# A convolution on TensorE in eight 64x32 tiles instead of four of full height, for the second 512 tokens of a fused convolution and gated network

## The chip, the cores and the metric

The kernel runs on one core of a Trainium2 chip. The metric is device time in microseconds for one launch, as the median over runs. A profile is one execution taken by the hardware profiler; its span runs from the first to the last instruction of the program.

## The reference

Eight sequences of 4096 tokens with 192 channels go through a causal depthwise convolution of seven taps, with the softmax of the weights as taps and one set of taps for each head of 24 channels. The result, 32768 tokens, goes through a gated network with 1536 hidden units.

```python
def _attn_ref(x, weight):
    ...                                   # w: softmax of weight over its 7 taps
    x_pad = np.concatenate([np.zeros((B, pad, D)), x], axis=1)      # pad = 6
    idx = np.arange(S)[:, None] + np.arange(K)[None, :]
    x_unf = x_pad[:, idx, :].reshape(B, S, K, H, group)
    out = np.einsum('hk,bskhg->bshg', w, x_unf)
    ...

def _moe_ref(x, w_gate, w_val, w_out):
    gate = np.maximum(x @ w_gate, 0.0)
    val = x @ w_val
    return gate * val @ w_out
```

## The kernel before

The kernel works on sixteen units of 1024 tokens, of two sequences at once (streams 0 and 1, in partitions 0 to 63 and 64 to 127), so a unit has two windows of 512 tokens. Three chunks of 64 channels (`NCH`) hold the 192 channels. For a window, `gate_val` goes over twelve blocks `f` of 128 hidden units: six matmuls with `Wg` and six with `Wv` (line 550), each half with the rows of one stream; then ACT takes the relu of the gate (line 561), and DVE multiplies with the value (line 562). The hidden activations are projected with `Wo` (lines 579, 628, 658) and written out.

The convolved tokens stand in `xc`. From unit 1 on DVE, ACT and POOL compute them in lanes, beside TensorE's work on the unit before. For unit 0 nobody had time, so TensorE does it: the stationary operand is a piece of raw tokens (`x_h`: tokens in partitions, channels along), the moving operand a band matrix (`band`) that holds the taps of one head along its diagonals. `first_block` convolves the first 512 tokens before the first products, `second_block` the second 512 tokens; the latter is called from `gate_val` between blocks 4 and 5 of the first window, so that PE meets it in program order right behind the matmuls of block 4. Both use `conv_dense` (line 370): a window is cut in five pieces of at most 104 tokens, which with six tokens of history fill 110 rows; for each chunk and piece there are two rounds of four matmuls, one for each 32 output channels (two streams, two halves of the chunk), at column places 0, 32, 64 and 96 of the array, all four into one PSUM bank. A second round is needed because 32 channels touch two heads: it overwrites the channels of the other head. So the block is 3 x 5 x 8 = 120 matmuls. ACT moves two chunks from PSUM to `xc` (line 394), DVE the third (line 396).

The order of instructions on each engine is the program's own: nothing reorders it (`tc.manual_schedule()`), and waits follow from data and buffers. PSUM is a pool of four tiles `ps` of two banks, used in turn by everything on TensorE.

POOL issues the transfers that change the type: tokens `x_h` for the first window (lines 134, 135), for the second (line 96, `load_x(1)`, one transfer per stream, two in all) and for the group behind (`load_x(2)`), weights `Wg` and `Wv` in six pieces (line 170). The weights arrive in partitions 0 to 63; DVE copies the first two pieces into partitions 64 to 127, POOL the others (lines 177 and 186). In POOL's order `load_x(1)` stands between pieces 2 and 3 of the weights. Piece 2 is for blocks 3 and 4, piece 3 for blocks 5 and 6, piece 4 for 7 and 8, piece 5 for 9 to 11. [...] Behind the weights POOL issues the raw tokens of unit 1 (line 208).

Of the kernel before, what the change touches and what calls it, by code (L numbers as in the profile page):

```python
# [17 lines left out]
def kernel(  # L18
# [12 lines left out]
    nc = tc.nc  # L31

    B, S, D = x.shape
    H, KW = weight.shape
    G = D // H
    DFF = moe_w_gate.shape[1]
    PAD = KW - 1
    NB = B // 2
# [3 lines left out]
    WIN = 512  # L42
    NWIN = S // WIN
    SUB = 112
# [2 lines left out]
    FOR_POOL = [(1, 6), (2, 6)]  # L47
    GSUB = 5
    DSUB = 104


    UNIT = 2 * WIN
# [4 lines left out]
    TDVE = (LDVE + HALO) // 128  # L57
    FIRST = WIN - DSUB * (GSUB - 1)
    GROUPS = [(0, [0] + [FIRST + DSUB * j for j in range(GSUB - 1)])]
    GROUPS += [(0, [WIN + DSUB * j for j in range(GSUB)])]  # L60
    GROUPS += [(0, list(range(UNIT + LDVE, 2 * UNIT, SUB)))]

    ctx.enter_context(tc.manual_schedule())
# [10 lines left out]
    psum = ctx.enter_context(tc.tile_pool(name="psum", bufs=4, space=bass.MemoryType.PSUM))  # L74
    dram = ctx.enter_context(tc.tile_pool(name="dram", bufs=2, space=bass.MemoryType.DRAM))

    ROOM = 4 * WIN

    def x_room():
        flat = xpool.tile([128, ROOM], F16, name="x_h")  # L80
        return flat[:, 0 : GSUB * 2 * D].rearrange("p (j s d) -> p j s d", j=GSUB, s=2)


    def load_x(g):


        bp, toks = GROUPS[g]
        n, rows, step = len(toks), SUB if g < 2 else 128, toks[1] - toks[0]
        xt = xts[g] = x_room()
        for st in range(2):  # L90
            src = bass.AP(
                tensor=x.tensor,
                offset=x.offset + ((bp + NB * st) * S + toks[0] - PAD) * D,
                ap=[[D, rows], [step * D, n], [1, D]],
            )
            nc.gpsimd.dma_start(out=xt[0:rows, 0:n, st, :], in_=src)
            yield
# [7 lines left out]
    xts = {}  # L105
    ROWS0 = DSUB + PAD
    SEG = 16
# [5 lines left out]
    def stage(p0, rows, st, n_st, jj, n):  # L113
        at = room[p0 : p0 + rows, 0, 0, 0:1]
        dims = [[D * GSUB, n_st], [D, n], [1, D]]
        return bass.AP(
            tensor=at.tensor,
            offset=at.offset + D * (GSUB * st + jj),
            ap=[at.ap[0]] + [d for d in dims if d[1] > 1],
        )  # L120

    xts[0] = x_room()

    def body(st):
        return bass.AP(
            tensor=x.tensor,
            offset=x.offset + (NB * st * S + FIRST - PAD) * D,
            ap=[[D, SUB], [DSUB * D, GSUB - 1], [1, D]],
        )
# [6 lines left out]
        out=xts[0][PAD : PAD + FIRST, 0, :, :],  # L136
        in_=bass.AP(
            tensor=x.tensor, offset=x.offset, ap=[[D, FIRST], [NB * S * D, 2], [1, D]]
        ),
# [35 lines left out]
    def both_halves(copy, s, dst):  # L175
        cols = slice(CUTS[s], CUTS[s + 1])
        copy(out=dst[64:128, :, cols], in_=dst[0:64, :, cols])
# [49 lines left out]
    load_w(1)  # L227
    load_w(2)
    load_rest(load_x(1))
    load_w(3)  # L230
    pool_parts(2)
# [9 lines left out]
    def bits(src, n, down, keep):  # L241
        out = const.tile([SUB, n], I32, name=f"bits{down}")
        nc.vector.tensor_scalar(
            out=out[:],
            in0=src,
            scalar1=down,
            scalar2=keep,
            op0=ALU.logical_shift_right,
            op1=ALU.bitwise_and,
        )  # L250
        return out
# [4 lines left out]
    col = bits(steps[:, 0:NROW], NROW, 0, 63)  # L256
# [3 lines left out]
    with nc.allow_low_precision("zero and one"):  # L260
        nc.vector.tensor_tensor(
            out=same[:], in0=col[:, 0:SEG], in1=s_of[:].to_broadcast([SUB, SEG]), op=ALU.is_equal
        )
        nc.vector.tensor_scalar(
            out=places[:, SUB - SEG : SUB - SEG + NROW],
# [7 lines left out]
        out=mx[:], in_=wr[:], axis=mybir.AxisListType.X, op=ALU.max, negate=True  # L273
# [6 lines left out]
    with nc.allow_low_precision("rounded as the band is"):  # L280
        nc.vector.tensor_scalar(
            out=soft[:],
# [7 lines left out]
        out=spread[0:SUB, 0, 0:H],  # L290
        lhsT=soft[:].rearrange("h k s -> h (k s)"),
        rhs=same[0:H, 0:H],
        start=True,
        stop=True,
# [3 lines left out]
    with nc.allow_low_precision("products with one and zero"):  # L298
        nc.vector.tensor_tensor(
            out=diag[:],  # L300
# [6 lines left out]
    for a in range(2):  # L307
        for b in range(NSEG):
            nc.tensor.matmul(  # L309
                out=(bps, spread)[a][:, a, HB * SEG * b : HB * SEG * (b + 1)],  # L310
                lhsT=places[:, SUB - SEG * (b + 1) : SUB - SEG * (b + 1) + 128],
                rhs=diag[:, HB * a : HB * (a + 1), :].rearrange("p h s -> p (h s)"),
                start=True,
                stop=True,
                skip_group_check=True,
# [4 lines left out]
    for cols in (slice(0, 64), slice(64, D)):  # L320
        nc.scalar.copy(
            out=xts[0][0:ROWS0, 1:GSUB, 0, cols],
            in_=stage(0, ROWS0, 0, 1, 1, GSUB - 1)[:, :, cols],
# [22 lines left out]
    def band(h):  # L346
        return bands[h]

    xc = {}
# [3 lines left out]
    def conv_dense(g, c, ps, bank):  # L353


        xt = xts[g]
        toks = GROUPS[g][1]
        t0 = toks[0]
        ends = toks[1:] + [t0 + WIN]
        for jj in (1, 2, 3, 4, 0):  # L360
            col, n = toks[jj] - t0, ends[jj] - toks[jj]
            rows = n + PAD
            for second in range(2):
                for st in range(2):
                    for k2 in range(2):
                        k = 2 * c + k2
                        h0, h1 = 32 * k // G, (32 * k + 31) // G
                        h, m = (h0, G * h1 - 32 * k) if second else (h1, 32)
                        p0 = 64 * st + 32 * k2
                        nc.tensor.matmul(  # L370
                            out=ps[p0 : p0 + m, bank, col : col + n],
                            lhsT=xt[0:rows, jj, st, 32 * k : 32 * k + m],
                            rhs=band(h)[0:rows, 0:n],
                            start=True,
                            stop=True,
                            tile_position=(0, p0),
                            skip_group_check=True,
                        )

    def first_block():  # L380
        xc[0] = xcpool.tile([128, NCH, UNIT], F16, name="xc")
        both_halves(nc.vector.tensor_copy, 0, Wg)
        both_halves(nc.vector.tensor_copy, 0, Wv)
        for c in range(NCH):
            ps = psum.tile([128, 2, 512], FP, name="ps")
            conv_dense(0, c, ps, 0)
            copy = nc.vector.tensor_copy if c == 2 else nc.scalar.copy
            copy(out=xc[0][:, c, 0:WIN], in_=ps[:, 0, :])

    def second_block():  # L390
        two, one = [psum.tile([128, 2, 512], FP, name="ps") for _ in range(2)]
        conv_dense(1, 0, two, 0)
        conv_dense(1, 1, two, 1)
        nc.scalar.copy(out=xc[0][:, 0:2, WIN : 2 * WIN], in_=two[:])
        conv_dense(1, 2, one, 0)
        nc.vector.tensor_copy(out=xc[0][:, 2, WIN : 2 * WIN], in_=one[:, 0, :])

    HEADS = (((0, 1), (3, 4)), ((6, 7), (2, 5)))

# [389 lines left out]


    first_block()
    taps = const.tile([H, KW], FP)
    nc.scalar.activation(taps[:], ex[:, 0:KW], ACTF.Copy, scale=sm[:])
    tap = const.tile([128, NCH, KW], FP)
    for h in range(H):
        r = G * h
        while r < G * (h + 1):
            c, n = r // 64, min(64 - r % 64, G * (h + 1) - r)
            nc.sync.dma_start(
                out=tap[r % 64 : r % 64 + n, c, :],  # L800
                in_=taps[h : h + 1, :].unsqueeze(1).to_broadcast([1, n, KW]),
# [8 lines left out]
    load_rest(lane_load(1))  # L810
    nc.gpsimd.tensor_copy(out=tap[64:128], in_=tap[0:64])
    load_rest(load_x(2))
    for end in ends:
        nc.gpsimd.memset(end, 0.0)
    load_rest(lane_turn(1))
    for u in range(NUNIT):
# [35 lines left out]
        if u + 1 < NUNIT:  # L852
            begun = lane_first(u + 1)
            if u == 0:
                flat = ypool.tile([128, ROOM], F16, name="y")
                y = flat[:, 0 : GSUB * NCH * 128].rearrange("p (j c s r) -> p j c s r", j=GSUB, c=NCH, s=2)
# [43 lines left out]
```

## Time and profile before

| what | value |
|---|---|
| median of 3 runs | 762.16 us (761.86 to 766.11) |
| span of the profiled execution | 759.9 us; its own time with what lies around the span isn't listed apart, the median of the runs is 2.2 us longer |
| PE busy | 756.1 us, 99% |
| DVE, ACT, POOL busy | 93%, 81%, 53% |
| first and second convolution on PE in the chain | 1.95 us and 1.62 us |
| unit 0 on PE | until 56.82 us |
| a later unit on PE | 46.6 us (from 56.82 to 103.56 us, for instance) |

A row of the timeline has the start in us, the length from the first start to the last end, the engine, the line, the operation, output and input, and how many instructions were merged. Brackets hold idle time of the engine before, and what ended it. PEld is the loading of the stationary operand, which runs beside PE. "Busy" of PE counts matmuls from start to a modelled end, and they overlap, so the spacing of starts says more than the duration of one.

### The profile page before, as it was taken

The numbers are of one execution on the slowest core, as the hardware profiler recorded it, in microseconds if no ns is written. First come the engines' busy times: TensorE is split into PE (matmuls) and PEld (weight loads), VectorE is DVE, ScalarE is ACT, GpSimd is POOL, SyncE is SP. The second block draws the span as 40 slices with busy tenths as digits, with TensorE's granted clock in tenths as the row PEclk, the third lists the DMA queues.
The fourth block names the chain that finished last, engine by engine and source line by source line (L and its number), as shares of the span: only waits on it lengthen the run. The fifth ranks groups of instructions, "written<-read, shape, count | busy, mean of one in ns | idle before, by whom it ended". The sixth has DMA issues, their size and how long they took to land.

```text
span 759.9 us, 30608 instructions
## 1 busy us (share of the span) xinstructions
PE 756.1 (99%) x13623; PEld 484.0 (64%) x13623; DVE 707.4 (93%) x768; ACT 617.3 (81%) x719; POOL 404.9 (53%) x263
## 2 busy tenths in 40 slices
PE   9999999999999999999999999999999999999998
PEld 5495555555666666666666666666666776666548
DVE  7998999999999999999999999999999999999891
ACT  6887887978879798897988879788798887976671
POOL 9519449094580936819276291863908548091000
PEclk9999999999999999999999999999999999999999
DMA  9969029688395894949759498594957939654732
GB/s 118 132 113 136 16 68 157 162 107 181 94 184 146 91 180 105 190 128 105 195 93 184 119 138 180 81 186 114 170 145 100 189 98 160 140 107 113 185 87 85
DMA packets 231308, 100.33 MB, mean 132 GB/s; under 512 B 185288, under 2 KB 220424, under 8 KB 231176
## 3 DMA queue, kind: packets, MB, share of 16 engines
q1 hardware_dynamic: 189928, 82.71, 53.1%
q0 software_dynamic: 41104, 15.57, 20.7%
q8 instruction: 106, 1.74, 1.0%
q14 instruction: 26, 0.21, 0.1%
q10 hardware_dynamic: 144, 0.10, 0.0%
HBM read 31.48 MB, written 47.19 MB: 104 GB/s over the span
## 4 chain that ended last, share of the span: by engine, by line
PE 99%; ACT 0%; issue 0%
PE ps L550 66%; PE ps L658 29%; PE ps L579 3%; PE ps L628 1%; PE ps L154 0%; PE ps L370 0%; PE ps L309 0%; PE ps L411 0%; ACT acc L605 0%; PE ps L289 0%
## 5 line engine op out<-in xcount | busy, mean ns | idle before, releaser
L562 DVE TENSOR_TENSOR hT<-gr,ps 128x1024 f16<-128x1024 f16 (+1 forms) x386 | 469.0, 1216 | 30.0 <-ACT gr L561 3.3
L561 ACT ACTIVATE gr<-ps 128x1024 f16<-128x1024 f32 (+1 forms) x386 | 393.3, 1020 | 100.7 <-PE ps L550 100.3
L498 POOL TENSOR_TENSOR prods<-prods 128x1344 f32<-128x1344 f32 x70 | 212.9, 3042 | 268.7 <-DVE prods L494 265.3
L550 PE MATMUL ps<-xc,Wg 64*64 64x512 f16 (+1 forms) x4320 | 321.9, 376 | 0.0
L550 PE MATMUL ps<-xc,Wv 64*64 64x512 f16 (+1 forms) x4320 | 321.6, 376 | 0.0
L658 PE MATMUL ps<-hT,Wo 64*64 64x512 f16 x4032 | 220.3, 376 | 0.0
L550 PEld LDWEIGHTS <-Wg 64*64 64x64 f16 (+1 forms) x4320 | 154.0, 106 | 94.9 <-issue 0.7
L550 PEld LDWEIGHTS <-Wv 64*64 64x64 f16 (+1 forms) x4320 | 152.7, 105 | 95.8 <-issue 0.3
L658 PEld LDWEIGHTS <-Wo 64*64 64x64 f16 x4032 | 140.2, 107 | 77.4
L522 DVE SCALAR_TENSOR_TENSOR acc<-x_r,tap,acc 128x576 f32<-128x576 f16 x225 | 165.3, 814 | 0.0
L492 ACT ACTIVATE prods<-x_r,tap 128x448 f32<-128x448 f16 x222 | 127.2, 659 | 0.0
L680 ACT COPY x_h<-ps 128x2048 uint16<-128x2048 uint16 x28 | 51.8, 1848 | 8.8 <-PE ps L658 8.8
L208 POOL DMA_DIRECT2D x_e<-in_x_dram x58 | 46.9, 818 | 12.3 <-ACT acc L508 12.0
L472 POOL COPY x_p<-x_e 128x960 f16<-128x960 f16 (+1 forms) x58 | 50.5, 912 | 0.5 <-DMA x_e<-in_x_dram 0.5
L498 POOL TENSOR_TENSOR xc<-prods 128x1344 f16<-128x1344 f32 x14 | 42.5, 3037 | 1.1
L680 POOL COPY y<-x_h 128x2048 uint16<-128x2048 uint16 x14 | 26.6, 1897 | 23.3 <-ACT x_h L736 23.3
L522 DVE SCALAR_TENSOR_TENSOR xc<-x_r,tap,acc 128x576 f16<-128x576 f16 x45 | 34.1, 813 | 0.0
L508 ACT ACTIVATE acc<-x_r,tap 128x576 f32<-128x576 f16 x45 | 31.4, 765 | 0.0
L494 DVE TENSOR_SCALAR prods<-x_r,tap 128x448 f32<-128x448 f16 x70 | 27.7, 448 | 0.0
L579 PE MATMUL ps<-Wo,hT 64*128 64x192 f16 x576 | 24.6, 243 | 0.0
L579 PEld LDWEIGHTS <-hT 64*128 64x128 f16 x576 | 23.9, 94 | 0.5
L736 ACT COPY x_h<-ps 128x512 f32<-128x512 f32 x14 | 8.2, 587 | 10.9 <-ACT x_h L680 5.5
(62 smaller groups left out, 91.6 us busy)
## 6 DMA issues: line engine op xcount, KB each, us to landing
out_dram<-out_s SPq DMA_DIRECT2D x62, 384.0 KB
held<-x_h SPq DMA_DIRECT2D x14, 512.0 KB
held<-x_h SPq DMA_DIRECT2D x28, 256.0 KB
held<-y SPq DMA_DIRECT2D x14, 512.0 KB
x_e<-in_x_dram POOLq DMA_DIRECT2D x34, 192.0 KB, 6.7
x_e<-in_x_dram POOLq DMA_DIRECT2D x24, 240.0 KB, 5.4
x_r<-x_p SPq DMA_TRANSPOSE x131
out_s<-held SPq DMA_TRANSPOSE x56
```

The costliest lines, as they stand in the source:

```text
L208: first = nc.gpsimd.dma_start(out=xe[:, j0 + start : j0 + n, st, :, :].rearrange("p j c r -> p j (c r)"), in_=bass.AP(tensor=x.tensor, off ...
L472: nc.gpsimd.tensor_copy(out=xp[:, j0 : j0 + n, :, st, :], in_=xe[:, j0 : j0 + n, st, :, :])
L492: engine.activation(out=out, in_=in_, func=ACTF.Copy, scale=scale)
L498: nc.gpsimd.tensor_tensor(out=pr[:, 0] if k < KW - 1 else xc[v + 1][:, :, LDVE:UNIT], in0=pr[:, 0], in1=pr[:, k], op=ALU.add,)
L508: nc.scalar.activation(out=accs[v][:, c, :], in_=shifted(v, c, 0, 0), func=ACTF.Copy, scale=tap[:, c, 0:1],)
L522: nc.vector.scalar_tensor_tensor(out=xc[v][:, c, 0:LDVE] if k == KW - 1 else acc[:, c, :], in0=shifted(v, c, k, 0), scalar=tap[:, c, k : k ...
L550: nc.tensor.matmul(out=pss[i][m : m + M, st, :], lhsT=W[64 * st : 64 * st + 64, c, 128 * f + m : 128 * f + m + M], rhs=xcb[64 * st : 64 * ...
L561: nc.scalar.activation(out=gr[:, sts], in_=pss[0][:, sts], func=ACTF.Relu)
L562: nc.vector.tensor_tensor(out=h[:, f, sts], in0=gr[:, sts], in1=pss[1][:, sts], op=ALU.mult)
L579: mm = nc.tensor.matmul(out=outs[q], lhsT=h[64 * r : 64 * r + 64, f, st, 128 * q : 128 * (q + 1)], rhs=Wo[64 * r : 64 * r + 64, f, :], sta ...
L658: mm = nc.tensor.matmul(out=ps[bank][64 * half : 64 * half + 64], lhsT=Wo[64 * r : 64 * r + 64, f, d : d + 64], rhs=hs[w][64 * r : 64 * r ...
L680: copy(out=pt[:], in_=src[:].bitcast(U16).rearrange("p b (t l) -> p b l t", l=2))
```

## The change

The second window is cut in six pieces of 43 tokens in each half of 256 tokens. A piece with its history is 49 rows, and the two halves stand in partitions 0 to 48 and 64 to 112 of one buffer. For each chunk and piece there are two rounds of eight matmuls, four column places times two row halves. Row half 0 writes into bank 0, row half 1 into bank 1, so a PSUM tile holds the first 256 tokens of two chunks in one bank and the last 256 in the other. The moving operand for row half 1 is the band matrix from its row 64 and column 64 on, which has the same diagonals. That is 3 x 6 x 16 = 288 matmuls, and 288 loads. The two copies out of PSUM read and write in strips of 256 tokens. `load_x(1)` issues four transfers, one per stream and half. The buffers for raw tokens grow from 2048 to 2304 elements per partition.

```diff
+    HSUB, NHS = 43, 6
+    HROWS = HSUB + PAD
...
-    GROUPS += [(0, [WIN + DSUB * j for j in range(GSUB)])]
+    GROUPS += [(0, [WIN + HSUB * j for j in range(NHS)])]
...
-    ROOM = 4 * WIN
+    ROOM = NHS * 2 * D
...
         xt = xts[g] = x_room()
+        if g == 1:
+            for st in range(2):
+                for r in range(2):
+                    src = bass.AP(
+                        tensor=x.tensor,
+                        offset=x.offset + (NB * st * S + toks[0] + WIN // 2 * r - PAD) * D,
+                        ap=[[D, HROWS], [step * D, n], [1, D]],
+                    )
+                    nc.gpsimd.dma_start(out=xt[64 * r : 64 * r + HROWS, 0:n, st, :], in_=src)
+                yield
+            return
...
+    def conv_split(c, ps, col0):
+        xt = xts[1]
+        for jj in range(NHS):
+            n = min(HSUB, WIN // 2 - HSUB * jj)
+            col = col0 + HSUB * jj
+            for second in range(2):
+                for st in range(2):
+                    for k2 in range(2):
+                        k = 2 * c + k2
+                        h0, h1 = 32 * k // G, (32 * k + 31) // G
+                        h, m = (h0, G * h1 - 32 * k) if second else (h1, 32)
+                        p0 = 64 * st + 32 * k2
+                        for r in range(2):
+                            rows = slice(64 * r, 64 * r + n + PAD)
+                            nc.tensor.matmul(
+                                out=ps[p0 : p0 + m, r, col : col + n],
+                                lhsT=xt[rows, jj, st, 32 * k : 32 * k + m],
+                                rhs=band(h)[rows, 64 * r : 64 * r + n],
+                                start=True,
+                                stop=True,
+                                tile_position=(64 * r, p0),
+                                skip_group_check=True,
+                            )
...
     def second_block():
         two, one = [psum.tile([128, 2, 512], FP, name="ps") for _ in range(2)]
-        conv_dense(1, 0, two, 0)
-        conv_dense(1, 1, two, 1)
-        nc.scalar.copy(out=xc[0][:, 0:2, WIN : 2 * WIN], in_=two[:])
-        conv_dense(1, 2, one, 0)
-        nc.vector.tensor_copy(out=xc[0][:, 2, WIN : 2 * WIN], in_=one[:, 0, :])
+        half = WIN // 2
+        conv_split(0, two, 0)
+        conv_split(1, two, half)
+        nc.scalar.copy(
+            out=xc[0][:, 0:2, WIN : 2 * WIN].rearrange("p c (r t) -> p c r t", r=2),
+            in_=two[:].rearrange("p r (c t) -> p c r t", c=2),
+        )
+        conv_split(2, one, 0)
+        nc.vector.tensor_copy(
+            out=xc[0][:, 2, WIN : 2 * WIN].rearrange("p (r t) -> p r t", r=2), in_=one[:, :, 0:half]
+        )
```

On POOL, between pieces 1 and 4 of the weights, before (sizes are partitions x runs x elements; `x2` counts equal rows in a row):

```order
L170 DMA Wg<-in_moe_w_gate_dram 64x3x256
L170 DMA Wv<-in_moe_w_val_dram 64x3x256
L96 DMA x_h<-in_x_dram 112x5x192 x2
L170 DMA Wg<-in_moe_w_gate_dram 64x3x256
L170 DMA Wv<-in_moe_w_val_dram 64x3x256
L177 COPY Wg<-Wg 64x3x256
L186 COPY Wv<-Wv 64x3x128 x2
```

and now:

```order
L183 DMA Wg<-in_moe_w_gate_dram 64x3x256
L183 DMA Wv<-in_moe_w_val_dram 64x3x256
L100 DMA x_h<-in_x_dram 49x6x192 x4
L183 DMA Wg<-in_moe_w_gate_dram 64x3x256
L183 DMA Wv<-in_moe_w_val_dram 64x3x256
L190 COPY Wg<-Wg 64x3x256
L199 COPY Wv<-Wv 64x3x128 x2
```

Two more token transfers, each with about half as many rows, stand ahead of piece 3 of the weights and of the copies of piece 2; the rest of POOL's order is as before.

On PE, the start of the second convolution behind block 4 (a matmul reads the band and the loaded tokens; the size is output channels x tokens), before:

```order
L550 MATMUL ps<-xc,Wv 128x512
L370 LDWEIGHTS x_h
L370 MATMUL ps<-band_182,x_h 32x104
L370 LDWEIGHTS x_h
L370 MATMUL ps<-band_182,x_h 32x104
```

and now:

```order
L595 MATMUL ps<-xc,Wv 128x512
L409 LDWEIGHTS x_h
L409 MATMUL ps<-band_184,x_h 32x43
L409 LDWEIGHTS x_h
L409 MATMUL ps<-band_184,x_h 32x43
```

The place in PE's order is the same; four such pairs made a round, and now eight pairs do, with 43 columns for 104. PE has 168 matmuls and 168 loads more in all.

More of the change, by code (lines that the diff above doesn't have):

```diff
@@ L75 @@
     dram = ctx.enter_context(tc.tile_pool(name="dram", bufs=2, space=bass.MemoryType.DRAM))
-    ROOM = 4 * WIN
+    ROOM = NHS * 2 * D
     def x_room():
         flat = xpool.tile([128, ROOM], F16, name="x_h")
-        return flat[:, 0 : GSUB * 2 * D].rearrange("p (j s d) -> p j s d", j=GSUB, s=2)
+        return flat[:, 0 : NHS * 2 * D].rearrange("p (j s d) -> p j s d", j=NHS, s=2)
     def load_x(g):
         bp, toks = GROUPS[g]
-        n, rows, step = len(toks), SUB if g < 2 else 128, toks[1] - toks[0]
+        n, rows, step = len(toks), 128, toks[1] - toks[0]
         xt = xts[g] = x_room()
+        if g == 1:
[9 more added lines that the diff above has]
+            return
         for st in range(2):
```

## The prediction

> **What bounds the kernel now.** I read the page first: engine shares and the chain that ended last.
>
> ```profile
> span 759.9 us, 30608 instructions
> PE 756.1 (99%) x13623; PEld 484.0 (64%) x13623; DVE 707.4 (93%) x768; ACT 617.3 (81%) x719; POOL 404.9 (53%) x263
> PE 99%; ACT 0%; issue 0%
> ```
>
> TensorE is the bound from end to end. The other engines matter only where they make PE wait, and PE never catches up a delay, since it has next to no idle time. So the question is local: when does PE leave the changed block and what follows it? The chain in order of time (start, length, what) shows its place:
>
> ```profile
> 7.23 6.74 PE ps L550 x60
> 13.97 1.62 PE ps L370 x113
> 15.59 24.71 PE ps L550 x228
> 56.82 31.20 PE ps L550 x576
> ```
>
> The changed convolution (L370, second call) is 1.62 us of 759.9, 0.2%. No saving in it can exceed that. The timeline of the first 22 us has its neighbours: gate and value products L550 of blocks 3 and 4 (Wg, then Wv), the convolution, block 5, and the Wv half of block 9.
>
> ```profile
> 11.09 0.94 PE L550 MATMUL ps<-xc,Wg 64*128 64x512 f16 x6
> 11.74 0.94 PE L550 MATMUL ps<-xc,Wv 64*128 64x512 f16 x6
> 12.39 0.94 PE L550 MATMUL ps<-xc,Wg 64*128 64x512 f16 x6
> 13.10 0.87 PE L550 MATMUL ps<-xc,Wv 64*128 64x512 f16 x6
> 13.90 1.69 PE L370 MATMUL ps<-band,x_h 110*32 110x104 f16 x120
> 15.07 1.01 ACT L394 CAST xc<-ps 128x1024 f16<-128x1024 f32 x1 [0.68 <-PE ps L370]
> 15.53 0.82 PE L550 MATMUL ps<-xc,Wg 64*128 64x512 f16 x6
> 15.68 0.69 DVE L396 CAST xc<-ps 128x512 f16<-128x512 f32 x1
> 16.18 0.81 PE L550 MATMUL ps<-xc,Wv 64*128 64x512 f16 x6
> 21.36 0.81 PE L550 MATMUL ps<-xc,Wv 64*128 64x512 f16 x5
> ```
>
> In the same stretch POOL issues the token transfer (L96) and, behind it on the same queue, the weight transfers (L170) and the copies of weights into partitions 64 to 127 (L177, L186), which PE needs:
>
> ```profile
> 6.06 0.63 POOL L170 DMA_DIRECT2D Wv<-in_moe_w_val_dram  x1
> 6.68 1.64 POOL L96 DMA_DIRECT2D x_h<-in_x_dram  x2
> 8.31 0.65 POOL L170 DMA_DIRECT2D Wg<-in_moe_w_gate_dram  x1
> 9.63 0.82 POOL L177 COPY Wg<-Wg 64x768 f16<-64x768 f16 x1
> 10.97 0.95 POOL L186 COPY Wv<-Wv 64x384 f16<-64x384 f16 x2 [0.52 <-DMA Wv<-in_moe_w_val_dram]
> 11.87 0.64 POOL L170 DMA_DIRECT2D Wg<-in_moe_w_gate_dram  x1
> 13.76 0.82 POOL L177 COPY Wg<-Wg 64x768 f16<-64x768 f16 x1
> 14.53 0.83 POOL L177 COPY Wv<-Wv 64x768 f16<-64x768 f16 x1
> 19.63 1.16 POOL L177 COPY Wv<-Wv 64x1152 f16<-64x1152 f16 x1
> 20.73 0.88 POOL L208 DMA_DIRECT2D x_e<-in_x_dram  x1
> ```
>
> The reader should compare ends with starts: the Wg copy for blocks 3 and 4 ends at 9.63 + 0.82 = 10.45, PE wants it at 11.09, a slack of 0.64 us. The last Wv copy ends at 20.79 and is wanted at 21.36, a slack of 0.57.
>
> **Term 1, the matmuls.** Before: 120 matmuls of up to 104 columns in the 1.62 us of the chain (13.90 to 15.52 in the timeline), 30 steps of four column tiles. What a column costs comes from the long rows: 576 matmuls of 512 columns in 31.20 us are 54 ns each, with four 64x64 tiles at work 217 ns for 512 columns, 0.42 ns a column. (That row also shows two row halves at work together, each into its own bank.) A step of 512/5 = 102 columns on average is then 43 ns, 30 of them 1.30 us; the other 0.32 us is entry, exit and tiles drifting apart. After: 3 x 6 x 2 = 36 steps of eight tiles, 288 matmuls and as many loads. By columns a step would take 43 x 0.42 = 18 ns. But the instructions must also start:
>
> ```profile
> L370 PEld LDWEIGHTS <-x_h x240: 82/93/147, 5.2 to 15.3; 110*32 110x32 f16 x49, 110*24 110x24 f16 x16, 110*8 110x8 f16 x16, 110*16 110x16 f16 x15
> L370 PE MATMUL ps<-band,x_h x240: 203/209/291, 5.2 to 15.4; 110*32 110x104 f16 x46, 110*24 110x104 f16 x16, 110*8 110x104 f16 x16, 110*16 110x104 f16 x16
> 13.90 0.11 PEld L370 LDWEIGHTS <-x_h 110*32 110x32 f16 x8 [0.42 <-issue]
> 13.90 0.23 PE L370 MATMUL ps<-band,x_h 110*32 110x104 f16 x4
> ```
>
> At 13.90 eight loads of 93 ns lie within 110 ns and four matmuls start among them: 12 starts in some 20 ns, 1.7 to 2 ns each. A step of eight has 16 starts, 27 to 32 ns. I take 30: start-bound, not column-bound. 36 x 30 = 1.08, plus the same 0.32, is 1.40 us: **0.22 us saved**. Bounds: 27 ns a step saves 0.33. On the other side the rows show a 32-column load hidden under a 43 ns step, not under less; if each step still lasts 43 ns, the block takes 1.55 + 0.32 = 1.87, 0.25 lost. I take 30 because the loads start as close together as the matmuls do.
>
> [...]
>
> **Term 2, two more transfers on POOL.** Two issues of 112x5 = 560 rows took 1.64 us, 0.82 each; an issue of 64x3 = 192 rows takes 0.62 from start to start (6.06 to 6.68). The change has four of 49x6 = 294 rows; by rows between the two, 0.68, less the overlap of neighbours, 0.67. 4 x 0.67 - 1.63 = 1.07 us later for everything behind (bounds: four at 0.62, 0.85 later; four at 0.82, 1.65 later). The Wg copy then runs from 10.70 to 11.52, and block 3 wants it at 11.09: **PE loses 0.43 us** (bounds 0.21 and 1.01). Of this 0.06 comes back: block 4's Wv already starts 0.71 behind its Wg, where 0.65 is usual, so it had a wait that now falls away. Net 0.37. The following Wv copy had waited 0.52 for its transfer, issued ahead of the tokens; that wait goes, so POOL is only 0.55 late after it. The next copies end at 15.13 and 15.91 (wanted near 15.68 and 16.33) and the last at 21.34, wanted after 21.36: nothing more is lost. If that cover were gone, each 0.1 us on POOL would be 0.1 us on PE.
>
> **Term 3, the landing of the tokens.** The view of DMA, first the transfer issued at 7.52, then the load on the engines from 9.5 to 13.2 us:
>
> ```profile
> x_h<-in_x_dram POOLq DMA_DIRECT2D x1, 210.0 KB, 5.7
> DMA packets 1569, 0.58 MB, mean 156 GB/s; under 512 B 1226, under 2 KB 1569, under 8 KB 1569
> q0 software_dynamic: 1440, 0.58, 131.5%
> ```
>
> The second transfer lands at 13.2, and the queue is full: 1440 packets in 3.7 us are 41 ns per packet on each of 16 engines. There are 4 x 294 = 1176 rows for 1120, 3.5 more per engine if spread evenly, 0.14 us: 13.3. PE wants them at 13.90 + 0.37 = 14.27. **Nothing**, with 0.9 us of cover.
>
> **Edits at no cost.** The ACT copy (1.01) and the DVE copy (0.69) move as many elements, in strips of 256 columns from two banks. ACT ended at 16.08, block 6 needs the bank one block, 1.30 us, behind 15.53. A copy twice as long would cost up to 0.5. The larger token buffer moves addresses only. Unit 1 is covered too:
>
> ```profile
> 40.62 2.10 ACT L508 ACTIVATE acc<-x_r,tap 128x576 f32<-128x576 f16 x3
> 41.94 3.20 POOL L208 DMA_DIRECT2D x_e<-in_x_dram  x4 [11.99 <-ACT acc L508]
> ```
>
> POOL stands idle for 12 us before 41.94 until ACT's first products, which 0.55 us does not reach. Beyond 42 us only PE's own delay is left.
>
> **The sum.** 759.9 - 0.22 + 0.37 = 760.05 us of span. The runs' median, 762.16, lies 2.2 us above the profiled span, so **762.3 us**: no change that could be measured (1%, 7.6 us, is about what a measurement of this kernel can tell from no change).
>
> **Rivals.**
>
> *The copies run later than I say.* Issues at 0.82 each, or the weight transfers behind the tokens landing late, put PE 0.6 to 1.6 us behind: 762.8 to 763.8. For it: the slacks of 0.64 and 0.57 are small against 1.65. Against: issues get shorter with fewer rows. 0.20.
>
> *The rows go to few engines (the slower side).* [...] 0.08. [...]
>
> *The row halves take turns.* 72 steps of 30 to 43 ns, 2.2 to 3.1 us plus 0.32: with term 2, 1.3 to 2.2 us slower, 763.5 to 764.4. Against: L550 does overlap its halves. 0.09.
>
> *Each step drains before the next.* A load and a matmul in full, 93 + 209 = 302 ns, for 36 steps: 10.9 us, 9.3 more, 771.8. Against: the 120 matmuls of before didn't. 0.05.
>
> *More is saved.* The four issues cost no more than 0.85 together and the step is 27 ns: 0.33 saved, 0.15 lost, 0.2 us faster, 762.0. 0.08.
>
> **How the numbers follow.** My forecast, 761.9 to 762.7, has 0.48, and 0.02 is left for something faster than anything in these rows. All cases but the draining steps stay within 1%: same 0.93, slower 0.05, faster 0.02. The range runs from 761.2 (0.3 saved, and as far below the lowest run, 761.86, again) to 765.2 (half of the few-engines case, and most of the runs' own scatter to 766.11); some 0.1 stays outside.
>
> **What would show it.** Right: 288 matmuls of the convolution within 1.3 to 1.6 us; four token issues of 0.6 to 0.75 us; block 3's second row half waiting some 0.4 us for POOL's Wg copy; block 5 starting between 15.4 and 15.9; unit 1 starting (56.82) within 0.5 us of before. Wrong: PE waiting for the token transfer, a convolution over 2 us, or any difference that grows after 57 us.

## The result, and the profile after

The changed kernel takes 771.81 us (median of 6 runs, 770.75 to 772.63) against 762.38 (6 runs, 761.86 to 766.11): a ratio of 1.012, 95% interval 1.011 to 1.0131. It is 9.4 us slower, all of it in and around a block that had taken 1.62 us. The ratios here and below are over all runs, and since a few runs of the kernel before took 765 to 770 us, they come out a little lower than the ratios of the medians.

From the page of the changed kernel: the span, the engines, the granted clock in 40 slices and two DMA queues (packets, MB, share).

```profile
span 769.1 us, 30948 instructions
PE 759.5 (99%) x13791; PEld 493.2 (64%) x13791; DVE 707.4 (92%) x768; ACT 617.4 (80%) x719; POOL 406.3 (53%) x265
PEclk9899999999999999999999999999999999999999
q0 software_dynamic: 42704, 15.60, 20.0%
q8 instruction: 108, 1.77, 1.0%
```

The span is 9.2 us longer, PE only 3.4 us busier: the rest is time in which PE does nothing. One slice of the clock, the second (19 to 38 us), shows 8 where before had 9 in all forty:

```profile
PEclk9999999999999999999999999999999999999999
```

The chain in order of time (start, length, what) puts it in one place:

```profile
14.90 1.54 PE ps L409 x144
16.44 2.33 issue
18.77 1.25 PE ps L409 x118
20.02 2.75 issue
23.04 26.44 PE ps L595 x228
65.99 31.20 PE ps L595 x576
```

Against the rows of before: the convolution starts at 14.90 for 13.97 (**0.93 us** late); it lasts 8.14 us for 1.62 (**6.52 more**), 5.08 of these in two pauses marked "issue", in which PE waited for nothing that the profile shows; the 228 products behind it take 26.44 us for 24.71 (**1.73 more**). The sum is 9.18. Unit 1 starts at 65.99 for 56.82, 9.17 later, and its 576 matmuls last 31.20 us in both. Nothing is added after that.

The timeline of PE from 12 us on shows where in the program the pauses fall; the bracket has the idle time before a row and what ended it:

```profile
12.14 0.82 PE L595 MATMUL ps<-xc,Wg 64*128 64x512 f16 x5 [0.69 <-POOL Wg L190]
14.83 1.61 PE L409 MATMUL ps<-band,x_h 49*32 49x43 f16 x147
18.77 1.25 PE L409 MATMUL ps<-band,x_h 49*32 49x43 f16 x128 [2.33 <-issue]
22.77 0.26 PE L409 MATMUL ps<-band,x_h 47*32 47x41 f16 x13 [2.75 <-issue]
22.97 1.46 PE L595 MATMUL ps<-xc,Wg 64*128 64x512 f16 x6
```

PE runs 147 pairs of load and matmul, pauses 2.33 us, runs exactly 128 pairs, pauses 2.75 us, and runs the last 13. 128 pairs are 256 instructions. The page's instruction queue, q8, moved 1.77 MB in 108 packets: 16 KB a packet, and 2 x 13791 instructions over 108 are 255 a packet. So a packet holds as many instructions as PE runs between its pauses. The row of the kernel before had been:

```profile
q8 instruction: 106, 1.74, 1.0%
```

When the packets moved is on record too. These are q8's rows in the changed kernel from 16.1 us to the end of the first pause (18.77), and from 19.8 us to the end of the second (22.77):

```profile
q8 instruction: 1, 0.02, 2.8%
q8 instruction: 1, 0.02, 2.9%
```

That is one packet in each stretch, and by these shares they took 1.2 and 1.4 us. In the trace they start at 16.15 and 19.88, and PE goes on 1.4 and 1.5 us behind the end of each, 2.6 and 2.9 us after its start.

Stretches of PE's time (busy time and count of PE, PEld, DVE, ACT, POOL; then the granted clock, the DMA share, GB/s):

```profile
14.83:18.77 3.94, 1.61 (x149) 1.42 (x148) 1.66 (x2) 0.48 (x1) 3.65 (x5) 1.00 0.82 99
18.77:19.69 0.92, 0.92 (x114) 0.91 (x114) 0.00 (x0) 0.33 (x1) 0.92 (x2) 1.00 0.66 99
19.69:22.77 3.08, 0.33 (x36) 0.21 (x23) 0.00 (x0) 0.69 (x1) 3.08 (x4) 0.50 0.86 83
22.97:26.65 3.68, 3.68 (x31) 1.36 (x20) 1.52 (x2) 1.02 (x1) 3.68 (x6) 0.52 1.57 185
26.65:40.00 13.35, 13.35 (x126) 6.49 (x124) 11.81 (x11) 10.43 (x11) 4.10 (x9) 1.00 0.87 122
```

The granted clock falls to 0.50 at 19.69 us, 0.92 us after the first pause and before the second, stays there through the second pause (0.52 over the stretch behind it), and is back at 1.00 from 26.65. The 18 products that start from 22.97 to 26.65 take 3.68 us, where at 108 ns each they would take 1.94: half clock costs 1.7 us, the third term.

POOL's rows (start, length, engine, what) hold the first:

```profile
6.68 3.29 POOL L100 DMA_DIRECT2D x_h<-in_x_dram  x4
11.26 0.82 POOL L190 COPY Wg<-Wg 64x768 f16<-64x768 f16 x1
```

Four issues at 0.82 us each, as much as an issue of 560 rows before; the copy for blocks 3 and 4 starts at 11.26 for 9.63.

### The profile page after: what moved, and what is told of

The parts are those of the page before. It is cut to its first block, busy times and chain, and to the rows that moved or that the text cites. A ratio compares the mean times of both kernels' runs of the same rounds, so it can differ in the third digit from the quotient of the medians.

```text
span 769.1 us, 30948 instructions
## 1 busy us (share of the span) xinstructions
PE 759.5 (99%) x13791; PEld 493.2 (64%) x13791; DVE 707.4 (92%) x768; ACT 617.4 (80%) x719; POOL 406.3 (53%) x265
## 3 DMA queue, kind: packets, MB, share of 16 engines
q8 instruction: 108, 1.77, 1.0%
## 4 chain that ended last, share of the span: by engine, by line
PE 97%; POOL 1%; issue 1%; ACT 0%; POOLq 0%
PE ps L595 64%; PE ps L703 28%; PE ps L624 3%; PE ps L673 1%; POOL x_h L100 0%; PE ps L409 0%; POOL Wg L183 0%; POOL Wv L183 0%; POOL x_h L147 0%; POOL Wg L190 0%; POOL x_h L148 0%; PE ps L456 0%; ACT acc L650 0%; POOL steps L146 0%; POOLq L146 0%
## 5 line engine op out<-in xcount | busy, mean ns | idle before, releaser
L595 PEld LDWEIGHTS <-Wg 64*64 64x64 f16 (+1 forms) x4320 | 157.6, 106 | 93.3 <-issue 1.7
L703 PEld LDWEIGHTS <-Wo 64*64 64x64 f16 x4032 | 143.6, 107 | 74.0
```

Source lines behind the costliest of these rows:

```text
L595: nc.tensor.matmul(out=pss[i][m : m + M, st, :], lhsT=W[64 * st : 64 * st + 64, c, 128 * f + m : 128 * f + m + M], rhs=xcb[64 * st : 64 * ...
L703: mm = nc.tensor.matmul(out=ps[bank][64 * half : 64 * half + 64], lhsT=Wo[64 * r : 64 * r + 64, f, d : d + 64], rhs=hs[w][64 * r : 64 * r ...
```

## The experiments

Theory A says that the pauses are the instruction supply: PE's instructions arrive in packets of 256, a new one takes some 4 us from PE's side (18.77 to 22.77 in the changed kernel), and a program that runs 256 in less goes dry. The rivals put the pauses in what is new about the tiles or the transfers.

| kernel | changed from | pairs in the block | pauses in PE's issue near it, us | median, us | ratio (95%) |
|---|---|---|---|---|---|
| e1_cut_columns | before | 288, four tiles of full height | 1.69, 2.50 | 770.68 | 1.0098 (1.0075 to 1.0121) |
| e2_spread | after | 3 x 96, apart | none | 764.69 | 1.0017 (0.9998 to 1.0037) |
| e3_two_later | after | 288 | 0.67, 5.26 | 772.38 | 1.0121 (1.0105 to 1.0138) |
| e4_64_partitions | after | 288 | 3.35, 3.83 | 771.18 | 1.0111 (1.0089 to 1.0133) |
| e5_four_transfers | before | 120 | none | 762.77 | 0.9996 (0.9976 to 1.0015) |
| e6_wo_later | after | 288 | 2.65, 2.21 | 771.24 | 1.0106 (1.0065 to 1.0147) |
| e7_144 | before | 144 | 1.89, in the products behind | 764.19 | 1.0017 (0.9998 to 1.0036) |
| e8_192 | before | 192 | 2.03 | 766.89 | 1.0054 (1.0035 to 1.0074) |

The kernel before had a median of 762.48 us beside e1 to e4 and 762.41 beside e5 to e8. Theory A's forecast of the time held for e1, e2, e4, e7 and e8 (in e1 the first pause, 1.69 us, is shorter than the 2 to 3 named); e3 came out 0.4 us above its range of 769 to 772.

### e1_cut_columns: 288 pairs without row halves

The kernel before, with the columns of a piece cut in two or three: as many matmuls and loads as the change, but four column tiles over 110 rows, one bank, two transfers.

```diff
+            parts = 1 if g == 0 else 3 if jj < 2 else 2
+            cuts = [n * i // parts for i in range(parts + 1)]
+            for a0, a1 in zip(cuts, cuts[1:]):
...
-                            out=ps[p0 : p0 + m, bank, col : col + n],
+                                out=ps[p0 : p0 + m, bank, col + a0 : col + a1],
...
-                            rhs=band(h)[0:rows, 0:n],
+                                rhs=band(h)[0:rows, a0:a1],
```

> The kernel before, with nothing of the change but the number of matmuls: the pieces of the second convolution keep 110 rows, one bank and two token transfers, and each is cut along its columns into two or three parts, so 288 matmuls and 288 loads stand where 120 did. Theory A (instruction stream): TensorE's instructions arrive in packets of 16 KB, 1.74 MB in 106 packets for 27246 instructions, 257 each, and a block that uses up a packet sooner than the next one can be fetched stands still; then this kernel pauses twice for 2 to 3 us in the block, comes back to the halved clock, and takes 6 to 9 us more than before, 768 to 771. Rival B (row halves: two banks, two halves of the array in turn): no pause, 288 starts at 8 ns, at most 0.8 us more, 762.2 to 763.2. Rival C (the four token transfers hold PE up): no pause, the same 762.2 to 763.2.

Measured 770.68 us. The timeline of PE:

```profile
14.34 1.93 PE L373 MATMUL ps<-band,x_h 110*32 110x34 f16 x147
17.96 1.23 PE L373 MATMUL ps<-band,x_h 110*32 110x52 f16 x128 [1.69 <-issue]
21.69 0.30 PE L373 MATMUL ps<-band,x_h 110*32 110x35 f16 x13 [2.50 <-issue]
```

The same 147, 128 and 13 pairs with pauses between, with neither row halves, nor eight tiles, nor a second bank, nor two more transfers. The count of instructions alone makes most of the loss, 8.2 of the 9.4 us. The 128 pairs take 1.23 us, like the change's 1.25, and in both traces they start 8.2 ns apart, though the tiles are other ones: in these two traces the spacing is per pair, not per step of tiles. The 147 pairs ahead are wider apart, 11.9 ns here and 9.7 in the change.

### e3_two_later: the block two blocks further on

```diff
-            if u == 0 and w == 0 and f == 5:
+            if u == 0 and w == 0 and f == 7:
                 second_block()
```

> The changed kernel, with the convolution ahead of product block 7 in place of 5, so 48 instructions later in PE's program and 2.6 us later. Theory A: PE runs dry at the same places of the program, so the first pause comes 24 pairs earlier within the convolution, after some 123 of them where it was after 147, and the second again 128 pairs behind; time 769 to 772. Rival B: the pauses stay at the same pairs of the convolution, after 147. Rival C: the tokens have long landed by then, no pause, 763 to 765.

Measured 772.38 us. The timeline of PE:

```profile
18.64 1.15 PE L409 MATMUL ps<-band,x_h 49*32 49x43 f16 x123
20.46 1.21 PE L409 MATMUL ps<-band,x_h 49*24 49x43 f16 x128 [0.67 <-issue]
26.93 0.45 PE L409 MATMUL ps<-band,x_h 49*8 49x43 f16 x37 [5.26 <-issue]
```

Two blocks of 12 pairs now stand ahead of the convolution, and 147 - 24 = 123: the pauses stay at fixed places of PE's program, while the convolution's own data and tiles have moved. This is the sharpest evidence for A. The first pause is shorter; that the products ahead leave the supply more time fits, but isn't shown by itself. The second is 5.26 us for the changed kernel's 2.75; why it is that long is open.

### e7_144 and e8_192: fewer extra pairs

As e1, with one or three pieces of a chunk cut in two, 144 and 192 pairs.

```diff
# e7
+            parts = 1 if g == 0 else 2 if jj == 0 else 1
# e8
+            parts = 1 if g == 0 else 2 if jj < 3 else 1
```

> The kernel before, with one piece of each chunk cut in two: 144 matmuls in the second convolution in place of 120, full height, two transfers. Instruction stream: no pause inside the convolution, but PE runs dry at the same place of the program as in the cut kernel with 288, which is now 3 pairs into product block 5, some 2.1 us sooner than the kernel before gets there, and stands there 1.5 to 2.5 us: 764 to 766.5. If only long bursts of convolution matmuls stall, 24 more of them cost 0.1 to 0.3 us: 762.5 to 762.8.

> The same with three pieces of each chunk cut in two: 192 matmuls. Instruction stream: exactly one pause, after 147 pairs, of 1.7 to 3 us, then the last 45 pairs, and no second, since the next place is 83 pairs further on, in the products, where 128 pairs last 7 us; a halved clock for 3.4 to 7 us behind it: 765 to 768. Without it: 0.3 to 0.5 us more, 762.8 to 763.

Measured 764.19 and 766.89 us. The timeline of PE, e7 first:

```profile
13.89 1.77 PE L373 MATMUL ps<-band,x_h 110*32 110x104 f16 x144
15.59 0.60 PE L553 MATMUL ps<-xc,Wg 64*128 64x512 f16 x3
18.09 0.60 PE L553 MATMUL ps<-xc,Wg 64*128 64x512 f16 x3 [1.89 <-issue]
```

and e8:

```profile
13.91 1.93 PE L373 MATMUL ps<-band,x_h 110*32 110x52 f16 x147
17.88 0.55 PE L373 MATMUL ps<-band,x_h 110*32 110x52 f16 x45 [2.03 <-issue]
```

Two stretches of products right behind the pause, laid out as above with the granted clock third from the end, first e7's, then e8's:

```profile
18.09:22.00 3.91, 3.91 (x37) 2.00 (x39) 2.14 (x2) 2.73 (x3) 3.91 (x5) 1.00 0.74 77
```

```profile
18.36:21.50 3.14, 3.14 (x27) 1.27 (x20) 1.38 (x2) 1.02 (x1) 3.14 (x4) 0.57 0.74 72
```

In e7 PE runs dry 3 pairs into the products of block 5, 144 + 3 = 147, at an ordinary matmul of 512 columns: the pause needs no convolution there. In e8 there is one pause after 147 pairs; then 45 short pairs in 0.48 us and products follow, 27 of them in the 3.14 us shown, and no second pause comes. The loss grows by steps, as A has it: +1.8, +4.5 and +8.2 us (e1) over 762.41 and 762.48. Behind e8's pause the clock was 0.57 over the 3.14 us shown (0.50 from 18.8 to 22.2 us, worked out from this stretch and the next, 0.96 from 21.50 to 30.00); behind e7's, 0.14 us shorter, it stayed at 1.00.

The kernel before stands near the edge. Its packet would be used up 147 - 120 = 27 pairs behind its convolution, 15.59 + 27 x 0.108 = 18.5 us by its 228 products in 24.71 us, and in e7 PE could go on at 18.09: an estimated 0.4 us to spare.

### e2_spread: the three chunks apart

The change with one chunk each ahead of blocks 5, 8 and 11, every chunk in its own PSUM tile.

```diff
+    SPREAD = (5, 8, 11)
+    def second_part(c):
+        ps = psum.tile([128, 2, 512], FP, name="ps")
+        conv_split(c, ps, 0)
+        copy = nc.vector.tensor_copy if c == 2 else nc.scalar.copy
...
-            if u == 0 and w == 0 and f == 5:
-                second_block()
+            if u == 0 and w == 0 and f in SPREAD:
+                second_part(SPREAD.index(f))
```

> The changed kernel, with the three chunks of the convolution apart, ahead of product blocks 5, 8 and 11, each into a PSUM tile of its own; the same 288 matmuls in row halves, the same four transfers. Theory A (instruction stream): 192 instructions at once, then three product blocks (72 instructions in 3.9 us) in which the next packet arrives: no pause, no halved clock; left are 0.9 us from the later weight copies and 0.6 to 1.4 us for three chunks of 0.75 to 1.0 us, 763.5 to 764.8. Rival B (row halves) and rival C (transfers): the pauses stay with the matmuls or the tokens, 768 or more.

Measured 764.69 us. The chain has the chunks, and a stretch of 16 us over all three the clock behind the five engines:

```profile
14.93 1.12 PE ps L409 x95
20.05 0.86 PE ps L409 x92
24.90 0.85 PE ps L409 x96
14.00:30.00 16.00, 16.00 (x409) 8.36 (x407) 12.70 (x11) 11.31 (x13) 14.75 (x23) 1.00 1.15 135
```

With products between the chunks no pause is left, the clock stays at 1.00, and 7.1 of the 9.4 us are gone. What remains is the change without its supply problem, and it is still no gain: 1.12 + 0.86 + 0.85 = 2.83 us for 1.62, 1.21 more, and POOL's delay of 0.96 (the first chunk at 14.93 for 13.97). The two make 2.2, and so do the medians (764.69 for 762.48).

### e6_wo_later: the DMA engines idle during the second refill

The transfer of `Wo`, which runs beside the pauses, moved behind the raw tokens of unit 1.

```diff
     pool_halves(4)
-    nc.gpsimd.dma_start(out=Wo[:], in_=moe_w_out.rearrange("(c p) d -> p c d", p=128))
...
     load_rest(lane_turn(1))
+    nc.gpsimd.dma_start(out=Wo[:], in_=moe_w_out.rearrange("(c p) d -> p c d", p=128))
```

> The changed kernel, with the transfer of Wo (576 KB, first needed at some 50 us) issued behind the lane copies of unit 1, some 10 us later, so that it is not on the DMA engines while TensorE's second packet is fetched. If the data on the engines are what makes a refill last 4 us: the first pause stays at 2.0 to 3.4 us, the second shrinks from 2.75 to 1.0 to 1.9 us, 769 to 771. If a refill lasts 4 us in any case: the second pause stays at 2.5 to 3 us, 771 to 772.5.

Measured 771.24 us. PE's timeline, then the DMA engines from 18 to 23 us in 40 slices of 0.125 us, and the instruction queue in that stretch:

```profile
14.83 1.60 PE L409 MATMUL ps<-band,x_h 49*32 49x43 f16 x147
19.07 1.24 PE L409 MATMUL ps<-band,x_h 49*32 49x43 f16 x128 [2.65 <-issue]
22.53 0.26 PE L409 MATMUL ps<-band,x_h 47*32 47x41 f16 x13 [2.21 <-issue]
GB/s 37 12 6 25 160 203 197 203 184 148 6 0 0 0 0 0 0 131 0 0 0 0 0 0 0 0 0 0 0 0 0 0 0 0 0 0 0 0 0 18
q8 instruction: 1, 0.02, 1.2%
```

The lone 131 marks the start of the 16 KB packet, near 20.2 us, with nothing else moving (131 GB/s for 0.125 us are its 16 KB, all counted in the slice in which it starts); its own time, 1.2% of 16 engines' 5 us, is about 0.95 us. PE had gone on at 19.07 and goes on again at 22.53. So with idle DMA engines the cycle still takes 3.46 us: 1.1 until the packet starts, 0.95 for the packet, 1.4 from its end until PE goes on. In the changed kernel the cycle was 4.00 (18.77 to 22.77) and the packet 1.4. Contention is worth some 0.5 us between these two traces, most of it in the packet itself; the rest passes in e6 as well, where from 19.4 us until PE goes on the packet is alone on the engines. The second pause, 2.21 us, lies between the two forecasts. The first pause was not relieved (2.65 for 2.33), and the median is 0.6 us lower, inside both intervals.

### e5_four_transfers and e4_64_partitions: the issues on POOL

e5 is the kernel before with its tokens in four transfers of 49 and 63 partitions; e4 is the change with 64 partitions loaded in each (15 rows unused).

```diff
# e5
+            if g == 1:
+                for p0, p1 in ((0, 49), (49, rows)):
...
+                    nc.gpsimd.dma_start(out=xt[p0:p1, 0:n, st, :], in_=src)
# e4
-    HROWS = HSUB + PAD
+    HROWS = 64
```

> The kernel before, with its own convolution of 120 matmuls, but with the tokens of the second window in four transfers, 49 and 63 rows of partitions for each stream. This is the change's cost on POOL alone. If an issue to a number of partitions that is no multiple of 16 costs 0.8 us whatever its rows: 1.6 us more on POOL, PE waits 0.8 to 1.0 us for the Wg copy of blocks 3 and 4, nothing else moves, 763.2 to 763.6. If, as the prediction had it, issues go by rows (245 and 315): 1.1 us more on POOL, PE loses 0.4, 762.8.

> The changed kernel, with 64 rows in each of the four token transfers in place of 49 (the 15 more are not used). On the transfers: if the 49 partitions are what makes an issue of 294 rows as long as one of 560 (0.82 us), an issue of 384 rows takes 0.68 to 0.72, POOL is 0.4 to 0.5 us less late, the 1544 more packets of 4 bytes go away, and PE's wait for the Wg copy of blocks 3 and 4 shrinks from 0.9 to some 0.4 us. If a transfer to a part of the partitions costs 0.8 in any case, nothing changes. Theory A: the two pauses in the convolution stay, so the time stays at 770.8 to 772. Rival C (landing of the tokens): the pauses change with the transfers.

e5 measured 762.77 us, 0.4 over the kernel before. That is the second forecast, 762.8, but the interval holds no difference at all, so the timing can't tell. Its trace can, and for 49 and 63 partitions it bears out the first. POOL and PE, then the chain:

```profile
6.66 3.46 POOL L103 DMA_DIRECT2D x_h<-in_x_dram  x4
12.33 0.82 PE L560 MATMUL ps<-xc,Wg 64*128 64x512 f16 x5 [0.81 <-POOL Wg L187]
15.09 1.48 PE ps L380 x120
16.57 24.71 PE ps L560 x228
```

3.46 us for the issues, PE 0.81 us idle for POOL's copy, and the convolution and all behind it 1.0 to 1.1 us late: two more transfers alone make the delay that the change has ahead of its convolution. The products take 24.71, as before. Why the medians show 0.4 us where the two traces show 1.0 is open.

e4 measured 771.18 us. POOL, then a row of the page:

```profile
6.70 2.67 POOL L100 DMA_DIRECT2D x_h<-in_x_dram  x4
11.15 0.82 POOL L190 COPY Wg<-Wg 64x768 f16<-64x768 f16 x1 [0.56 <-DMA Wg<-in_moe_w_gate_dram]
q0 software_dynamic: 41552, 15.73, 20.3%
```

With more rows (384 for 294) an issue is cheaper, 0.67 us for 0.82, and the queue moves 1152 packets fewer than in the changed kernel. So the issue doesn't go by rows; 49 partitions cost more than 64. PE gets almost nothing of it: POOL's copy now waits 0.56 us for the weights' landing and starts at 11.15 for 11.26, and the convolution starts at 14.72 for 14.83, 0.1 us sooner where 0.4 to 0.5 was expected. The profiled execution of e4 took 773.32 us, 2.1 above the median, and its two pauses sum to 2.1 us more than the changed kernel's.

## Why the prediction was wrong

**The bound and the place were right.** PE is the bound, no engine catches a delay up, and all of the loss lies in the block and its neighbours. But "no saving in it can exceed 1.62 us" had no counterpart for a loss, and the loss was six times the block.

**The step that failed is term 1**, twice over.

- The 30 ns a step came from twelve starts at the head of a burst. They are real: the change's first 32 pairs come as close. This row is the stretch of the convolution's own PE and PEld rows in the changed kernel:

```profile
14.83:14.95 0.12, 0.12 (x32) 0.12 (x32) 1.00 1.21 162
```

 That is 3.7 ns a pair, 30 ns for eight, and it doesn't last: over the 147 pairs the starts are 9.7 ns apart, over the 128 behind the first pause 8.2, which is 66 to 77 ns for a step of eight. By that 36 steps are 2.4 to 2.8 us; e2's three parts, each with its own entry and exit, measured 2.83, 1.2 more than before. "Start-bound" was right; the start was priced at less than half.
- The supply of instructions had no term at all. Two pauses of 5.08 us, and the half clock behind them of 1.7, are 6.8 of the 9.2 us. The row "issue 0%" of the page before had shown that the supply kept up with products, 108 ns a pair around the block (24.71 us for 228), and with one block of 120 pairs; that a longer run would outpace it, no row of before could show directly, but the queue q8, 106 packets in all, and the count of instructions were on its page. The bounds of the term, from 0.33 saved to 0.25 lost, went by matmuls only.

**Term 2 had the right path and a wrong price.** Issues were priced by rows, 0.67; they took 0.82, the upper end named, and by e4 rows don't set it. PE lost 0.93 at the convolution's start, where 0.37 was forecast and 1.01 the bound. It is e5 that shows the cause.

**Term 3 and the edits at no cost held.** No row of PE waits for the tokens. The cover was thinner than the 0.9 us forecast: the fourth token transfer starts at 9.2 us and lands 5.3 us later, near 14.5, and PE's first matmul on the tokens starts at 14.83. The upper end of the range, 765.2, counts in half of the few-engines case, a term that no run shows; what the changed kernel showed in its place is these 0.3 us of cover and no wait. The two copies after the convolution take as long as before:

```profile
19.36 1.01 ACT L434 CAST xc<-ps 128x1024 f16<-128x1024 f32 x1 [4.05 <-PE ps L409]
23.12 0.69 DVE L439 CAST xc<-ps 128x512 f16<-128x512 f32 x1 [6.56 <-PE ps L409]
```

**The rivals.** "Each step drains" gave 771.8, within 0.1 us of the median, for a wrong reason: between the pauses the pairs overlap (128 in 1.25 us, where a drained step was 302 ns), and the pauses come after 147 and 128 pairs, not after each step of eight. "The row halves take turns" falls with e1, which has none and the same spacing of 8.2 ns; that its price, 2.5 to 3.4 us for the block, holds e2's 2.83 is chance. "The copies run later than I say" came true as a part, 0.93 us. Of the signs named beforehand, "a convolution over 2 us" is the one that appeared; no difference grew after 57 us.

**On the supply, page and trace.** The trace shows 16 KB packets, 255 instructions to a packet, and in the changed kernel a stop after 147 pairs and after 128 more, 256 instructions. In the kernel before, with 106 packets, the boundaries cost nothing that its page shows ("issue 0%" in the chain); with a run of short pairs ahead they cost 0.67 to 5.26 us each (both in e3).

What stays open: what sets the 8.2 ns a pair, why the first 147 are wider apart, what passes in the 2.5 us of a refill in which e6's packet isn't on the DMA engines, and why the second pause is 5.26 us in e3 and 3.83 in e4, where it is 2.75 in the changed kernel.

## What to carry to other kernels

Count instructions as well as columns: cutting one matmul into smaller ones is bounded by the spacing of starts in a long run (here 8.2 to 9.7 ns a pair in the changed kernel, not the 3.7 ns of its first 32), and in these runs PE ran dry where 256 of its instructions took 1.2 to 1.3 us, while from going on after the first pause to going on after the second it took 3.46 to 6.5 us. If short matmuls are needed, spread them between long ones, as e2 did (no pause, the clock at 1.00 from 14 to 30 us), since half clock can follow a pause (in e8 it followed one of 2.03 us). A transfer's issue on POOL had a price of its own here, not a share by rows (0.82 us with 294 rows, 0.67 with 384); look who stands behind it on that queue.

## What the runs showed of the hardware

- PE stopped in pauses marked "issue" at program places that don't move with the data (after 147 pairs, then after 128; after 123 when 24 pairs more stood ahead). From going on after the first pause to going on after the second it took 3.46 us in e6, with nothing but the packet on the DMA engines from 19.4 us on, 3.7 in e1, 4.0 in the changed kernel, 5.1 in e4 and 6.5 in e3. PE went on 2.6 and 2.9 us after the start of a packet in the changed kernel and 2.3 in e6.
- The granted clock fell to 0.50 at 0.92 us after a pause of 2.33 us and was back by 26.65 us, some 7 us later. In e8 it was 0.50 for 3.4 us after a single pause of 2.03 us; in e7, after one of 1.89 us, it stayed at 1.00.
- Over 128 pairs behind the first pause, load and matmul pairs started 8.2 ns apart, with four tiles of 110 rows (e1) as with eight of 49 (the change); the first 32 of the change's burst started 3.7 ns apart.
- A token transfer of 49 partitions took 0.82 us to issue with 294 rows, one of 64 partitions 0.67 with 384.
